# Other due times for the list scheduler of a one-core attention and two-layer kernel

## The chip, the core and the metric

The kernel runs on one core of one Trainium2 chip, as one program. The metric is the device time of that core in microseconds (us), the median over runs. A profile shows one execution: busy times of TensorE's matmuls (PE), of its weight loads (PEld), of VectorE (DVE), ScalarE (ACT), GpSimd (POOL), and of the DMA queue on SyncE (SP).

## The reference, cut to what matters

Sliding-window attention with a linear bias, and then two dense layers without any routing:

```python
B, H, S, D = 2, 8, 768, 64                       # q, k, v: float32
rel = pos[:, None] - pos[None, :]
keep = (pos[None, :] < 8) | ((rel >= 0) & (rel < 96))
scores = q @ k.T / 8 - slope[h] * dist           # dist: 96 for far global keys, else |rel|
a = softmax(where(keep, scores, -1e9))
x = (a @ v)  ->  1536 rows x 512
h = x @ w_in                                     # 512 x 2048
g = where(h >= 1, h, where(h <= -1, 0, (h + 1) ** 2 / 4))
x = g @ w_out                                    # 2048 x 512
h = x @ w_in2 ; g = maximum(0.01 * h, h) ; out = g @ w_out2
```

The weights arrive as 64-bit numbers, two 32-bit words each, and are put together on the chip.

## The kernel before

Every float32 operand of the dense layers is split into a high and a low part, `hi` and `lo`, and each product is taken as hi·hi, hi·lo and lo·hi. A hidden tile is 128 hidden units by up to 512 rows of `x`: 12 matmuls of 512 columns with the two parts of four pieces of 128.

The work is a list of operations. Each is put on it with `add(costs, fn, prio, after, takes, gives)`: what it would cost on each engine that may do it, the function that issues it, a priority, what must be done before, and the buffers that it takes from and gives back to rings. At build time `run()` (in `Schedule`) plays this list with the written costs: a free engine takes the ready operation with the smallest priority whose buffers are free, and its instructions are issued there and then. So the priority decides three things that stand fixed in the program afterwards: the order on each engine, which of several engines does an operation, and which buffer it gets. Where the player finds PE idle in the stretch up to the scores of the attention, it issues a dummy matmul on zeros (`dummy`, L369). Nothing is decided while the chip runs, except that an engine waits for what its next instruction needs.

The priority of an operation is a due time: the place of its tile in the play, plus an offset of its kind from the table `DUE` and some single constants:

```python
nms = [add({POOL: 2 * (pool_ts(W) + 83), DVE: 2 * (dve(W, True) + 62)}, nm(y), d + DUE["nm"] + y, [o7]) for y in range(2)]
due = due_of(c) + o * OUTLAG - JLEAD - (JTWO if m and not o else 0)
p2 = add({PE: c6}, prod(Ba, wa, 1, x0, 2, False, True), d + 2 * n7, [p1, cp, s_of[0, 2], s_of[0, 3]])
cc = add({DVE: dve(512)}, lambda e: V.tensor_tensor(out=Bc.tile, in0=Bb.tile, in1=S5.tile, op=ALU.add),
         d + 3 * n7 + 1400 + DUE["b0"], [p6, s5], ps=True)
p7 = add({PE: c6}, prod(Bb, wc, 0, lambda: xt[1], 0, False, False), d + 4 * n7, [cc] + x2_op["t3"])
```

The stages, and the names that come up again:

- **Attention**, 24 quads of four heads by 128 rows, `quad(i)`. PE transposes keys and queries (L559, `kd`, `qd`), the parts are taken from the bank (L220 or L222 for hi, L226 for lo), PE makes the scores (L591, `ks`, `qt`), VectorE adds the bias and finds the maximum (L600), ScalarE takes the exponent (L609), VectorE the reciprocal of the sum (L615), and the row is scaled, by VectorE (L622) or GpSimd (L624), which is operation `nm`. PE transposes the result (L633, `sm`) in two halves y = 0 and 1, and multiplies it with `v` (L646, `pT`, `vd`).
- **Weights**, `job(c, o)`: 16 tiles of `w_in` (o = 0) and of `w_out` (o = 1) for each layer, c = 0 to 31. A 512 KB load is followed by a chain that puts the words together: L438 or L440, L444, L448, L452 (VectorE alone; two inputs), L456 (ScalarE), L459 (a sum, VectorE or GpSimd), then the high part (L220 or L222) and the low part (L226 on VectorE, L228 on GpSimd).
- **Layer 1**, `step(s)`, 54 of them, the first ones between the quads: the hidden tile (L727), activation (L734, L742 or L744, L749), high and low part of the activated tile `g` (L220, and L226 or L228), the output product (L789).
- **Layer change**: the sums of layer 1 become the new `x`, and sums of its blocks become `xt` (L880, L226).
- **Layer 2**, `two(j, pair)`, j = 0 to 7, two weight tiles at a time. For two thirds of the rows seven products p1 to p7 stand in for eight (L921, 6 matmuls each), issued as p1, p5, p2, p6, p7, p3, p4. Between them a copy (cp, L220 or L222) is needed ahead of p2, a sum `cc` on VectorE (L966) ahead of p7, which also needs p6, and a second sum `ce` (L969) ahead of p4. The last third goes straight (L988). Activation is L932 and L937, the output product L1003, its sums L828, the last sums and the stores L846 and L849.

Of the kernel before, what the change touches and what calls it, by code (L numbers as in the profile page):

```python
# [55 lines left out]
class Schedule:  # L56
# [13 lines left out]
    def add(self, costs, fn, prio, after=(), takes=(), gives=(), tail=0.0, ps=False):  # L70

        o = Op()
        o.costs, o.fn, o.prio, o.gives, o.tail, o.ps = costs, fn, prio, gives, tail, ps

        o.takes = [(a, sum(b.ring is a.ring for b in takes[:y])) for y, a in enumerate(takes)]
        o.users, o.done, o.at = [], None, 0.0
        o.waits = 0
        for a in after:  # L80
            if a is not None and a.done is None:
                o.waits += 1
                a.users.append(o)
        self.ops.append(o)
        return o
# [91 lines left out]
def emit(tc, q, k, v, n_global, n_local, w_in1, w_out1, w_in2, w_out2, out, narrow):  # L177
# [25 lines left out]
    def act(n, psum=True):  # L203
        return (52 if psum else 93) + 0.833 * n

    def dve(n, fast=False):
        return 67 + (0.523 if fast else 1.044) * n
# [4 lines left out]
    def pool_ts(n):  # L212
        return 230 + 0.834 * n
# [10 lines left out]
    def sub(e, out_, a, b):  # L224
        if e == DVE:
            V.tensor_tensor(out=out_, in0=a, in1=b, op=ALU.subtract)  # L226
        else:
            GP.tensor_tensor(out=out_, in0=a, in1=b, op=ALU.subtract)  # L228

    def both(n):  # L230
        return {DVE: dve(n), POOL: pool_tt(n)}
# [48 lines left out]
    t_hid = []  # L280
    z = START
    units = PASSES[0]

    def quads(u):
        return range(u[0] // P * NQ, u[1] // P * NQ)

    for i in quads(units[0]):
        t_att[i] = START - STEP * (len(quads(units[0])) - i)
    for s, (m, g, u, f, first, last) in enumerate(seq):
        c = (u[1] - u[0]) * 10.15  # L290
        if m == 0 and g == 0 and u != units[-1]:
            after = quads(units[units.index(u) + 1])
            if first:
                seg = GROUPS[0] * c + len(after) * ATT
                for i in after:
                    t_att[i] = z + seg * (i - after[0] + 0.5) / len(after)
            c += len(after) * ATT / GROUPS[0]
        t_hid.append(z)
# [4 lines left out]
    t_two = []  # L303
    z -= TWO
    for j in range(NJ):
# [104 lines left out]
    def due_of(c):  # L410
        return t_hid[first_use[c]] if c < KF else t_two[(c - KF) // 2 * 2]

    jobs = sorted(((c, o) for c in range(NC) for o in range(2)), key=lambda j: (due_of(j[0]) + j[1] * OUTLAG, j[1]))
    w_t, w_op = {}, {}
    words = {}

    def job(c, o, prev):

        m, f = divmod(c, KF)
        due = due_of(c) + o * OUTLAG - JLEAD - (JTWO if m and not o else 0)  # L420
        R, Dd, Rr, W = Slot(raw), Slot(wd_r), Slot(wr_r), Slot(places[o])
# [42 lines left out]
        def s5(e):  # L464
            sub(e, W.tile[:, 1], Dd.tile.bitcast(F32), W.tile[:, 0].bitcast(F32))
        a = add({SP: 1460}, load, due + DUE["wl"], [prev], takes=[R], tail=DLAT)
        b = add({ACT: act(DM, False), DVE: dve(DM, True)}, s0, due + DUE["s0"], [a] + line("s0"), takes=[Dd])
        chain["s0"] = b
        b = add({POOL: pool_ts(DM), DVE: dve(DM, True)}, s01, due + DUE["s01"], [b])
        b = add({DVE: dve(DM, True)}, s1, due + DUE["s1"], [b])  # L470
        c1 = add({DVE: dve(DM)}, s11, due + DUE["s11"], [b])
        r = add({ACT: act(DM, False)}, s2, due + DUE["s2"], [a], takes=[Rr])
        e0 = add(both(DM), s3, due + DUE["s3"], [c1, r], gives=[Rr])
# [232 lines left out]
    def line(a):  # L706

        return [] if narrow else [chain.get(a)]
# [352 lines left out]
ABANKS = 6  # L1061
HBANKS = 3
SN = 1
JTWO = 4876.0
TWO = 6630.0
START = 547.0
STEP = 3638.0
ATT = 6076.0
OUTLAG = 10187.0
JLEAD = -3657.0  # L1070
DLAT = 2000.0

DUE = {'b0': 28848.0, 'b1': 29448.0, 'b2': 11048.0, 'b3': 11968.0, 'b4': -14334.0, 'bo': 42723.0, 'c1': 23764.0, 'c2': -19869.0, 'c3': -8113.0, 'c4': -7112.0, 'c5': -29972.0, 'c6': 58405.0, 'v': -15633.0, 'vg': 40229.0, 'a': -32879.0, 'half': 2.22, 'ld': -22756.0, 'tr': -4096.0, 'hi': -10213.0, 'lo': -27853.0, 'kg': -7231.0, 's': 12743.0, 'mx': -11641.0, 'ex': -9.0, 'rs': -70576.0, 'nm': -7377.0, 'ptr': -13975.0, 'pev': 10907.0, 'xmm': 9435.0, 'xhi': 9772.0, 'xlo': -2731.0, 'wl': -22500.0, 's0': -8192.0, 's01': -17963.0, 's1': 8642.0, 's11': -7299.0, 's2': 12279.0, 's3': 45224.0, 's4': -2838.0, 's5': -8589.0}


def load_words(nc, n_i, n_global, n_local):
# [140 lines left out]
```

## Time and profile before

| | |
|---|---|
| median of 3 runs | 622.96 us (622.67 to 623.07) |
| time of the profiled execution | 623.39 us |
| its span | 621.6 us |
| mean granted clock of TensorE in it | 0.997 |
| PE busy | 610.2 us, 98% of the span, 3404 matmuls |
| VectorE, ScalarE, GpSimd busy | 483.2, 352.6, 189.5 us |
| bytes moved | 46.98 MB |

The span runs from the first to the last instruction that the profile shows; the time holds 1.8 us more around it. PE is the engine that is nearly always busy, so time can be won or lost only where it waits, where it does work that isn't needed, or at the two ends of the program.

### The profile page before, as it was taken

The page shows a single profiled execution, that of the slowest core. Times are in us where ns is not written, and L with a number is a line of the kernel's source. Part 1 is how long each engine was busy: PE and PEld are TensorE (multiplying, and loading weights), DVE is VectorE, ACT ScalarE, POOL GpSimd, SP SyncE. Part 2 cuts the span into 40 slices and gives each one's busy share as a digit, 9 for nine tenths or more (in the row PEclk, how much of TensorE's full clock was granted, in tenths as well). Part 3 has the DMA queues.
Part 4 walks back from the last instruction along what each step waited for, and adds up shares of the span by engine and source line. Part 5 has one row for each costly group of instructions (what it writes and reads, how often), then busy time and mean ns, then how long its engine had stood idle before and what let it go on. Part 6 is the DMA issues. An engine that isn't in the chain of part 4 may idle for free.

```text
span 621.6 us, 9582 instructions
## 1 busy us (share of the span) xinstructions
PE 610.2 (98%) x3404; PEld 507.2 (82%) x3404; DVE 483.2 (78%) x1063; ACT 352.6 (57%) x755; POOL 189.5 (30%) x228
## 2 busy tenths in 40 slices
PE   9999999999999999999999999999999999999995
PEld 7888988888888888888888678888887888887884
DVE  6999899979994779823469999737989966988563
ACT  6999888966654456634445657524464533555300
POOL 3556634433220002200015052002545322556000
PEclk9999999999999999999999999999999999999998
DMA  9775344124331314400012103200232220220014
GB/s 188 191 171 128 84 129 99 46 69 135 106 114 54 101 35 141 131 1 1 0 35 67 35 34 103 67 1 1 67 108 80 85 67 2 68 69 1 2 59 150
DMA packets 61809, 46.98 MB, mean 76 GB/s; under 512 B 39608, under 2 KB 56248, under 8 KB 61752
## 3 DMA queue, kind: packets, MB, share of 16 engines
q1 hardware_dynamic: 61752, 46.28, 26.0%
q8 instruction: 29, 0.48, 0.3%
q14 instruction: 28, 0.23, 0.1%
HBM read 43.12 MB, written 3.15 MB: 74 GB/s over the span
## 4 chain that ended last, share of the span: by engine, by line


## 5 line engine op out<-in xcount | busy, mean ns | idle before, releaser
L789 PE MATMUL bank<-g,w 128*128 128x512 f32 (+1 forms) x648 | 141.7, 367 | 0.3 <-DVE g L226 0.3
L727 PE MATMUL bank<-x,w 128*128 128x512 f32 (+1 forms) x648 | 140.8, 367 | 0.4 <-DVE w L226 0.4
L789 PEld LDWEIGHTS bank<-g,w 128*128 128x128 f32 x648 | 112.3, 188 | 21.4 <-issue 0.9
L727 PEld LDWEIGHTS bank<-x,w 128*128 128x128 f32 x648 | 112.1, 188 | 21.2 <-DVE w L226 0.6
L828 DVE TENSOR_TENSOR part<-bank,part 128x512 f32<-128x512 f32 x96 | 63.6, 684 | 22.7 <-PE bank L1003 18.8
L1003 PE MATMUL bank<-w,g 128*128 128x512 f32 x312 | 80.5, 389 | 0.0
L459 POOL TENSOR_TENSOR wd<-wd,wr 128x512 int32<-128x512 int32 x36 | 49.6, 1377 | 87.5 <-DVE wd L452 73.0
L1003 PE MATMUL bank<-w,w 128*128 128x512 f32 x264 | 70.2, 389 | 0.0
L220 ACT CAST g<-t 128x512 fp32r<-128x512 f32 (+1 forms) x69 | 40.6, 591 | 49.3 <-PE bank L789 22.3
L1003 PEld LDWEIGHTS bank<-w,g 128*128 128x128 f32 x312 | 58.6, 188 | 12.2
L220 ACT CAST w<-wd 128x512 fp32r<-128x512 f32 x56 | 34.7, 620 | 45.2 <-POOL wd L459 12.4
L228 POOL TENSOR_TENSOR w<-wd,w 128x512 fp32r<-128x512 f32 x31 | 41.8, 1348 | 58.6 <-ACT w L220 32.6
L1003 PEld LDWEIGHTS bank<-w,w 128*128 128x128 f32 x264 | 49.5, 188 | 10.3
L734 ACT ACTIVATE t<-bank,half 128x512 f32<-128x512 f32 (+1 forms) x54 | 34.5, 640 | 41.3 <-PE bank L727 41.1
L226 DVE TENSOR_TENSOR g<-t,g 128x512 fp32r<-128x512 f32 (+1 forms) x60 | 42.2, 713 | 16.2 <-ACT g L220 16.0
L749 DVE SCALAR_TENSOR_TENSOR t<-bank,t 128x512 f32<-128x512 f32 (+1 forms) x54 | 33.8, 627 | 27.1 <-ACT t L742 26.6
L452 DVE SCALAR_TENSOR_TENSOR wd<-raw,wd 128x512 int32<-128x512 int32 x64 | 52.0, 812 | 1.5
L921 PE MATMUL bank<-x,w 128*128 128x512 f32 x192 | 48.4, 390 | 1.2 <-ACT bank L220 0.6
L444 POOL TENSOR_SCALAR wd<-wd 128x512 f32<-128x512 f32 x26 | 16.6, 643 | 107.0 <-ACT wd L438 93.2
L456 ACT ACTIVATE wr<-raw 128x512 int32<-128x512 uint32 x64 | 42.3, 670 | 11.9 <-DVE wd L459 10.7
L609 ACT ACTIVATE sm<-sm,st 128x256 f32<-128x256 f32 (+1 forms) x96 | 46.2, 489 | 0.1
L988 PE MATMUL bank<-x,w 128*128 128x512 f32 x192 | 45.1, 389 | 0.0
(115 smaller groups left out, 944.4 us busy)
## 6 DMA issues: line engine op xcount, KB each, us to landing
raw<-in_moe_w_in_dram SPq DMA_DIRECT2D x32, 512.0 KB, 3.7
raw<-in_moe_w_out_dram SPq DMA_DIRECT2D x32, 512.0 KB, 3.3
kd<-in_k_dram SPq DMA_DIRECT2D x24, 128.0 KB, 3.2
qd<-in_q_dram SPq DMA_DIRECT2D x24, 128.0 KB, 3.3
vd<-in_v_dram SPq DMA_DIRECT2D x12, 256.0 KB, 3.7
out_dram<-part SPq DMA_DIRECT2D x11, 256.0 KB, 2.1
out_dram<-part SPq DMA_DIRECT2D x2, 128.0 KB, 3.8
vg<-in_v_dram SPq DMA_DIRECT2D x2, 64.0 KB, 3.6
```

What stands on the lines that cost most here:

```text
L220: A.copy(out=out_, in_=in_)
L226: V.tensor_tensor(out=out_, in0=a, in1=b, op=ALU.subtract)
L452: V.scalar_tensor_tensor(out=Dd.tile, in0=hl()[0], scalar=-0x40000000, in1=Dd.tile, op0=ALU.bitwise_and, op1=ALU.bitwise_or)
L456: A.activation(out=Rr.tile, in_=hl()[1], func=AF.Copy, scale=2.0 ** -29)
L459: (V if e == DVE else GP).tensor_tensor(out=Dd.tile, in0=Dd.tile, in1=Rr.tile, op=ALU.add)
L609: A.activation(out=Sm.tile[:, a, 0:W], in_=Sm.tile[:, a, 0:W], func=AF.Exp, scale=-1.0, bias=St.tile[:, 0, a:a + 1], accum_out=St.tile[:, ...
L727: T.matmul(out=Hb.tile[:, 0:n], lhsT=wi.tile[:, a, kk * P:(kk + 1) * P], rhs=x[r][:, b, kk, c0:c0 + n], start=(kk == 0 and a + b == 0), st ...
L789: T.matmul(out=o[:, z * n:(z + 1) * n], lhsT=wo.tile[:, a, cc * P:(cc + 1) * P], rhs=Gt.tile[:, b, 0:n], start=st, stop=sp_)
L828: V.tensor_tensor(out=part[r][sl], in0=ac(), in1=part[r][sl], op=ALU.add)
L921: T.matmul(out=bank.tile, lhsT=w.tile[:, a, (2 * z + kk) * P:(2 * z + kk + 1) * P], rhs=xx()[:, b, kx + kk, :], start=st and kk == 0 and a ...
L988: T.matmul(out=Hb.tile, lhsT=w.tile[:, a, kk * P:(kk + 1) * P], rhs=x[2][:, b, kk, :], start=(kk == 0 and a + b == 0), stop=(kk == KD - 1 ...
L1003: T.matmul(out=Bo.tile, lhsT=Gt[z, r].tile[:, b, cb * P:(cb + 1) * P], rhs=wo[z].tile[:, a, :], start=(z == 0 and a + b == 0), stop=(z == ...
```

## The change

Only numbers of the table are replaced: seven single constants and the 41 offsets of `DUE`. No operation, cost, buffer ring or dependency is touched. The lines with single constants, and some of the offsets:

```diff
-JTWO = 4876.0
-TWO = 6630.0
-START = 547.0
-STEP = 3638.0
-ATT = 6076.0
-OUTLAG = 10187.0
-JLEAD = -3657.0
+JTWO = 5481.0
+TWO = 5365.0
+START = 1129.0
+STEP = 1441.0
+ATT = 6033.0
+OUTLAG = 9078.0
+JLEAD = -4197.0
```

What this does to the program is seen in the order of its instructions. In the pass that runs, PE has the same products, with 94 dummy matmuls in place of 90. VectorE has 27 instructions fewer, GpSimd 20 more, ScalarE 7 more. The order on PE differs up to about the 20th hidden tile of layer 1, is the same from there to the layer change, and differs again in parts of layer 2.

**First place: GpSimd, early in the attention.** The rows of GpSimd around the 30th; `sm` are the scores that `nm` scales (L624), `w_0_86` is the first tile of `w_in`, which the first hidden tile needs. Before:

```order
L624 TENSOR_SCALAR sm_124<-sm_124,st_127 128x256 x4
L222 CAST ks<-kg 128x4x32
L624 TENSOR_SCALAR sm_122<-sm_122,st_125 128x256 x4
L222 CAST ks<-kg 128x4x32
L459 TENSOR_TENSOR wd_82<-wd_82,wr_84 128x512
L624 TENSOR_SCALAR sm_124<-sm_124,st_127 128x256 x2
L744 TENSOR_TENSOR t_98<-t_98 128x256
```

After:

```order
L624 TENSOR_SCALAR sm_123<-sm_123,st_126 128x256 x2
L222 CAST ks<-kg 128x4x32
L459 TENSOR_TENSOR wd_82<-wd_82,wr_84 128x512
L222 COPY vd_116<-vg_118 32x512
L228 TENSOR_TENSOR w_0_86<-wd_82,w_0_86 128x512
L444 TENSOR_SCALAR wd_82<-wd_82 128x512
L624 TENSOR_SCALAR sm_122<-sm_122,st_125 128x256 x2
```

The low part of the first weight tile stood on VectorE (L226) and now stands on GpSimd (L228), with its sum (L459) earlier. The first hidden tile itself moves on PE from behind the sixth quad's product with `v` to behind the fourth's.

**Second place: VectorE at the layer change.** `g_95`, `g_96` and `g_97` are activated tiles of the last steps of layer 1, `w_1_91` is a weight tile, `t_98` and `t_99` are tiles in activation, `wd_82` a weight under way. L749 ends an activation and frees a bank. Before:

```order
L226 TENSOR_TENSOR xt_2100<-part_68,xt_2100 128x512 x2
L226 TENSOR_TENSOR w_1_91<-wd_82,w_1_91 128x512
L226 TENSOR_TENSOR g_97<-t_98,g_97 128x512
L226 TENSOR_TENSOR g_95<-t_99,g_95 128x512
L444 TENSOR_SCALAR wd_82<-wd_82 128x512
L448 TENSOR_SCALAR wd_82<-wd_82 128x512
L744 TENSOR_TENSOR t_98<-t_98 128x512
L749 SCALAR_TENSOR_TENSOR t_98<-bank_72,t_98 128x512
L749 SCALAR_TENSOR_TENSOR t_99<-bank_75,t_99 128x512
```

After:

```order
L226 TENSOR_TENSOR xt_2063<-part_68,xt_2063 128x512 x2
L226 TENSOR_TENSOR g_96<-t_99,g_96 128x512
L226 TENSOR_TENSOR g_95<-t_98,g_95 128x512
L226 TENSOR_TENSOR w_1_91<-wd_82,w_1_91 128x512
L744 TENSOR_TENSOR t_99<-t_99 128x512
L749 SCALAR_TENSOR_TENSOR t_99<-bank_77,t_99 128x512
L444 TENSOR_SCALAR wd_82<-wd_82 128x512
L749 SCALAR_TENSOR_TENSOR t_98<-bank_70,t_98 128x512
```

The two activated tiles now come ahead of the weight, and the first L749 ahead of the weight's next step. On ScalarE, at the same place, the copy cp and the last two activations of layer 1 now come ahead of weight steps.

**Third place: PE in the last pair, j = 7.** `x_66` and `xt` are the rows of the products (p6 is the row with `xt` and the weight `w_5`, p7 the next one with `xt`). Before:

```order
L921 MATMUL bank_71<-x_66,w_4_2102 128x512 x6
L921 MATMUL bank_70<-xt_2098,w_5_2103 128x512 x6
L1003 MATMUL bank_73<-w_2_92,g_94 128x512 x3
L1003 MATMUL bank_73<-w_7_2109,w_6_2108 128x512 x3
L921 MATMUL bank_70<-xt_2099,w_4_2102 128x512 x6
```

After:

```order
L921 MATMUL bank_71<-x_66,w_4_2065 128x512 x6
L921 MATMUL bank_70<-xt_2061,w_5_2066 128x512 x6
L1003 MATMUL bank_72<-w_0_90,w_3_93 128x512 x3
L1003 MATMUL bank_72<-w_1_91,g_97 128x512 x3
L1003 MATMUL bank_76<-w_0_90,w_3_93 128x512 x3
L1003 MATMUL bank_76<-w_1_91,g_97 128x512 x3
L921 MATMUL bank_70<-xt_2062,w_4_2065 128x512 x6
```

Between p6 and p7 there was one output product (six matmuls of L1003), and there are two now. In pair j = 4 two stand there before and after, but one further output product is moved ahead of that pair's p5.

## Rows read from the trace of the kernel before

**Rows 1.** The page: busy time by engine, with share of the span and count.
```profile
PE 610.2 (98%) x3404; PEld 507.2 (82%) x3404; DVE 483.2 (78%) x1063; ACT 352.6 (57%) x755; POOL 189.5 (30%) x228
```

**Rows 2.** Window of 40 to 60 us: length, busy (count) of PE, PEld, DVE, ACT, POOL, clock, DMA.
```profile
40.00:60.00 20.00, 19.00 (x197) 15.92 (x197) 19.72 (x77) 19.14 (x60) 10.59 (x19) 1.00 0.59 147
```

**Rows 3.** Timeline of PE, middle of layer 1: start, duration, engine, line, count.
```profile
253.87 2.88 PE L789 MATMUL bank<-g,w 128*128 128x512 f32 x12
256.58 2.88 PE L727 MATMUL bank<-x,w 128*128 128x512 f32 x12
```

**Rows 4.** Timeline, first hidden tile and quad 10; in brackets the idle time before.
```profile
42.12 0.50 PE L727 MATMUL bank<-x,w 128*128 128x256 f32 x2
43.06 1.45 PE L727 MATMUL bank<-x,w 128*128 128x256 f32 x10 [0.44 <-DVE w L226]
...
57.78 2.22 POOL L624 TENSOR_SCALAR sm<-sm,st 128x256 f32<-128x256 f32 x4 [3.54 <-DVE st L615]
57.91 0.67 PE L633 MATMUL bank<-ident,sm 128*128 128x128 f32 x4
59.13 0.66 PE L633 MATMUL bank<-ident,sm 128*128 128x128 f32 x4 [0.56 <-DVE x L226]
```

**Rows 5.** Timeline, layer change.
```profile
346.35 3.11 PE L789 MATMUL bank<-g,w 128*128 128x512 f32 x13
349.71 1.42 PE L789 MATMUL bank<-g,w 128*128 128x512 f32 x5 [0.26 <-DVE g L226]
350.98 1.53 PE L921 MATMUL bank<-x,w 128*128 128x512 f32 x6
351.70 1.29 DVE L749 SCALAR_TENSOR_TENSOR t<-bank,t 128x512 f32<-128x512 f32 x2
353.04 1.65 PE L921 MATMUL bank<-x,w 128*128 128x512 f32 x6 [0.54 <-DVE t L749]
354.69 0.57 ACT L220 COPY bank<-bank 128x512 f32<-128x512 f32 x1
355.32 1.65 PE L921 MATMUL bank<-x,w 128*128 128x512 f32 x6 [0.63 <-ACT bank L220]
...
359.53 2.88 PE L789 MATMUL bank<-g,w 128*128 128x512 f32 x12
362.80 1.65 PE L921 MATMUL bank<-xt,w 128*128 128x512 f32 x6 [0.38 <-DVE bank L966]
```

**Rows 6.** Timeline, pair j = 7, p6 and p7.
```profile
569.97 1.40 POOL L459 TENSOR_TENSOR wd<-wd,wr 128x512 int32<-128x512 int32 x1 [1.09 <-DVE wd L452]
570.25 1.66 DVE L452 SCALAR_TENSOR_TENSOR wd<-raw,wd 128x512 int32<-128x512 int32 x1
570.86 0.84 PE L1003 MATMUL bank<-w,w 128*128 128x512 f32 x3
571.84 0.68 DVE L966 TENSOR_TENSOR bank<-bank,s 128x512 f32<-128x512 f32 x1
572.58 1.65 PE L921 MATMUL bank<-xt,w 128*128 128x512 f32 x6 [0.88 <-DVE bank L966]
```

**Rows 7.** Timeline of PE, pair j = 4, between p6 and p7.
```profile
477.19 2.88 PE L1003 MATMUL bank<-w,g 128*128 128x512 f32 x12
480.20 1.67 PE L921 MATMUL bank<-xt,w 128*128 128x512 f32 x6
```

**Rows 8.** Timeline of PE, dummies and scores behind them; transposes and scores behind them.
```profile
7.25 2.02 PE L369 MATMUL bank<-zero 128*128 128x256 bf16 x17
9.19 1.32 PE L591 MATMUL bank<-ks,qt 64*128 64x256 f32 x12
...
44.35 1.04 PE L633 MATMUL bank<-ident,sm 128*128 128x128 f32 x8
45.31 0.86 PE L591 MATMUL bank<-ks,qt 64*128 64x256 f32 x10
```

**Rows 9.** Groups by line and shape: count, busy, mean ns of one, idle before.
```profile
L452 DVE SCALAR_TENSOR_TENSOR wd<-raw,wd 128x512 int32<-128x512 int32 x64 | 52.0, 812 | 1.5
```

More of the change, by code (lines that the diff above doesn't have):

```diff
@@ L1063 @@
 SN = 1
-JTWO = 4876.0
-TWO = 6630.0
-START = 547.0
-STEP = 3638.0
-ATT = 6076.0
-OUTLAG = 10187.0
-JLEAD = -3657.0
+JTWO = 5481.0
[5 more added lines that the diff above has]
+JLEAD = -4197.0
 DLAT = 2000.0
-DUE = {'b0': 28848.0, 'b1': 29448.0, 'b2': 11048.0, 'b3': 11968.0, 'b4': -14334.0, 'bo': 42723.0, 'c1': 23764.0, 'c2': -19869.0, 'c3': -8113.0, 'c4': -7112.0, 'c5': -29972.0, 'c6': 58405.0, 'v': -15633.0, 'vg': 40229.0, 'a': -32879.0, 'half': 2.22, 'ld': -22756.0, 'tr': -4096.0, 'hi': -10213.0, 'lo': -27853.0, 'kg': -7231.0, 's': 12743.0, 'mx': -11641.0, 'ex': -9.0, 'rs': -70576.0, 'nm': -7377.0, 'ptr': -13975.0, 'pev': 10907.0, 'xmm': 9435.0, 'xhi': 9772.0, 'xlo': -2731.0, 'wl': -22500.0, 's0': -8192.0, 's01': -17963.0, 's1': 8642.0, 's11': -7299.0, 's2': 12279.0, 's3': 45224.0, 's4': -2838.0, 's5': -8589.0}
+DUE = {'b0': 27487.0, 'b1': -7725.0, 'b2': 7698.0, 'b3': 18155.0, 'b4': -16724.0, 'bo': 42135.0, 'c1': 30472.0, 'c2': -36403.0, 'c3': -26250.0, 'c4': 9666.0, 'c5': -29309.0, 'c6': 42928.0, 'v': -18596.0, 'vg': 36984.0, 'a': -30449.0, 'half': 2.49, 'ld': -23578.0, 'tr': -1097.0, 'hi': -10704.0, 'lo': -25632.0, 'kg': -8445.0, 's': 6573.0, 'mx': -17624.0, 'ex': 167.0, 'rs': -86791.0, 'nm': -7267.0, 'ptr': -16954.0, 'pev': 11914.0, 'xmm': 6016.0, 'xhi': 12260.0, 'xlo': -7956.0, 'wl': -24180.0, 's0': -7248.0, 's01': -21914.0, 's1': 7880.0, 's11': -5575.0, 's2': 14164.0, 's3': 46641.0, 's4': -16435.0, 's5': 4613.0}
 def load_words(nc, n_i, n_global, n_local):
```

## The prediction

> **What bounds the kernel now.** I read the page's busy times first: PE works 98% of the span and VectorE 78%, so nothing but PE's own gaps can hold more than a per cent [rows 1]. Then I walked the timeline of PE from end to end and compared the distance between the starts of neighbouring blocks with what their matmuls need. In the middle of layer 1 twelve matmuls of 512 columns take 256.58 − 253.87 = 2.71 us, 0.226 each [rows 3]; a block whose distance to the next start is longer has waited by the difference. Idle time in brackets is less than that, since a pipelined PE drains while it waits.
>
> Seven waits come out of that walk, in four places, and nothing else above 0.2 us:
>
> - *First hidden tile*, 0.7: it starts at 42.12, does two matmuls, and goes on at 43.06 when VectorE has made the low part of its weight; 0.94 − 2 × 0.113 (256 columns) = 0.71 [rows 4].
> - *Quad 10*, 0.7: four transposes at 57.91, the next four at 59.13; at 0.12 each the first four need 0.48, so 0.74 is lost. The row blames VectorE's L226, but that is the last of several to signal; what the second half needs is `nm`, which GpSimd runs from 57.78 on [rows 4].
> - *Layer change*, four waits [rows 5]. 349.71 − 346.35 − 13 × 0.226 = 0.42, for the low part of an activated tile. 353.04 − 350.98 − 1.36 = 0.70, for p5, whose bank L749 gives back. 355.32 − 353.04 − 1.36 = 0.92, for p2, which needs the copy cp on ScalarE; about 0.13 of it is PE's restart after a stop (a block that starts after a stop lasts 1.65 and not 1.53). 362.80 − 359.53 − 2.71 = 0.56, for p7 and `cc`. With the restarts behind the first and the last (0.14 and 0.13) that is 2.87.
> - *Pair 4*, 0.4: 480.20 − 477.19 − 2.71 = 0.30, and 0.1 of a restart, p7 again [rows 7].
> - *Pair 7*, 1.15: 572.58 − 570.86 − 3 × 0.226 = 1.04 and 0.1 of a restart, p7 again: `cc` ran at 571.84 only, since the L452 ahead of it on VectorE lasted 1.66 [rows 6].
>
> Together 0.7 + 0.7 + 2.87 + 0.4 + 1.15 = 5.8 us, not quite 1% of the span. That is all a pure reordering can win from waits.
>
> **The change, part by part.** No operation is added or taken away but dummies, so every term is a wait that goes, stays or comes, or PE's own overhead.
>
> *The early attention.* The low part of the first weight stood on VectorE, which is busy 19.72 of 20 us there [rows 2]; now it is GpSimd's, with half of its time free, right behind its sum L459. PE meets the tile two quads earlier, which takes slack away again: between the two the low part is ready about a microsecond ahead by my count of GpSimd's work in the new order. `nm` of quad 10 goes to GpSimd alone, with a similar margin. I take both waits as gone: −1.4. If either comes back it costs its 0.7.
>
> *The layer change.* On VectorE the two low parts of `g` now stand ahead of the weight's. One L226 of 0.6 to 0.7 us leaves the way of the first wait of 0.42, which goes, with its restart: −0.56. p5 still needs its bank: the square of that step (L744) goes to GpSimd, which takes 1.40 for two inputs where VectorE takes 0.68 [rows 6], so L749 can't come much earlier. I leave 0.70 and add 0.3 and a restart: +0.4. The copy cp ran behind a weight's cast on ScalarE and started at 354.69; it now stands ahead of the weight's steps and can start when p1 is done. p1 ended by 352.51, p2 was due (without its wait) at 353.04 + 1.36 = 354.40, so 0.6 for the copy is covered: −0.92. `cc` waited for VectorE to clear a queue that is now shorter by a low part and two activations that GpSimd takes: −0.69. Sum −1.8; the bounds are 0 (all waits return in another form) and −2.87.
>
> *Pair 4.* One output product of six matmuls, 6 × 0.226 = 1.36 us, moves ahead of p5. VectorE and ScalarE have that much longer to prepare the pair's weights ahead of p6, and `cc` is not stuck behind them: −0.4, bounds 0 and −0.4.
>
> *Pair 7.* A second output product stands between p6 and p7, 1.36 us more of cover for a wait of 1.04: −1.15, with 0.3 to spare. If `cc` were held once more as long as there it would be late by about 0.7, so the lower bound of the gain is 0.4.
>
> *Dummies.* Four more, each (9.19 − 7.25) / 17 = 0.114 us [rows 8]: +0.45. Where PE would have waited anyway they cost nothing, so the bounds are 0 and 0.45; PE has no wait there in the trace of before, so I take the upper one.
>
> *Changes of the matmul's kind.* PE loses a little when the kind of tile changes: seven steps between transposes and the one to the scores take 45.31 − 44.35 = 0.96 [rows 8]; if seven take 0.11 like the dummies, the last is 0.2, some 0.1 too long. The new order has six such changes fewer (scores and products with `v` stand side by side more often): −0.6, bounds 0 and −0.6.
>
> *All other steps.* Some 60 instructions change their engine and nearly every quad has a new order. That every operation is on time again in such an order isn't to be hoped for. Bounds: nothing, and 5.8, as much as the order of before has. I take two waits of the mean size of the seven (5.8 / 7 = 0.83), rounded to +1.5.
>
> Sum: −1.4 − 1.8 − 0.4 − 1.15 + 0.45 − 0.6 + 1.5 = −3.4. The profiled execution took 623.39, which gives 620.0; it is 0.43 above the median of the runs shown, so the median should come to **619.6**.
>
> **One price weighed more closely.** The L452 of pair 7 began at 570.25, while GpSimd's L459 ran from 569.97 to 571.37, and lasted 1.66 [rows 6]. The mean of all 64 is 0.812 [rows 9], and one that meets nothing lasts about as long as the `cc` behind it, 0.68. So a two-input operation of VectorE that starts under one of GpSimd's is held for up to 0.98. The Trainium skill, page "SBUF — State Buffer", section "SBUF: two separate sides", says that VectorE and GpSimd share a pair of ports as an exclusive lock: whichever starts first has it for its whole instruction, and the other waits (VectorE when it has two inputs in SBUF against a GpSimd operation that reads SBUF). This row agrees: 1.66 is about the 1.12 left of L459 plus most of an own 0.68. It speaks against this change: by the rule the 20 instructions that go to GpSimd take VectorE's time as well as GpSimd's, up to the length of each, and the gain from moving them could turn into a loss; by the row that they are off VectorE's queue it couldn't.
>
> **Rivals.**
>
> *As many waits come as go.* For it: the new order is made by the same player from written costs, and the waits of before sit where a duration was not the written one (the L452 of 1.66). Nothing says that this happens less often in the new order. Against it: the walk through the new order shows cover at each of the old places. With 5.8 back in place of 1.5, the sum is +0.9 without margin to the dummies; with four or five new waits of 0.83 it is −4.9 + 4.5 × 0.83 = −1.2 to −0.4. I take −0.5, 622.5: no change that can be told.
>
> *Nothing comes in their place.* All named waits go and none comes: −4.9, a median of 618.1.
>
> *Slower: VectorE and GpSimd collide in the attention.* Place: 40 to 60 us, where VectorE has 0.28 us free in 20 and PE 1.0 [rows 2]. Each GpSimd operation with two inputs that now starts ahead of one of VectorE's may hold it for 0.98 us; with VectorE full, that delay goes on to every quad behind it until PE stops. Ahead of it is the margin of about a microsecond of the first tile and the 4.9 of terms that gain. Five collisions in the way of PE eat 4.9; from the seventh, 7 × 0.98 = 6.9, the kernel is 2 us slower than before, 625. Against it: scaling by `nm`, most of what moves in that stretch, has one input and no partner there, and of the 64 instructions of L452 together only 64 × (0.812 − 0.68) = 8.4 us are lost now in the whole kernel [rows 9], nearly all off the path.
>
> *The change does nothing.* That is the case of 622.5 by another road: PE is 98% busy, and the old waits may simply move by a block.
>
> **How the numbers follow.** A difference of 0.2%, 1.25 us, is about what a measurement of this kernel can tell from none. The forecast (618.6 to 621.5) gets 0.47; nothing in their place (617.5 to 618.6) 0.12; as many come as go (621.5 to 624.2) 0.26; slower by collisions 0.15. Faster by over 0.2% is below 621.7: 0.47 + 0.12 + 0.03 of the third = 0.62. Slower is above 624.2: 0.15. Same: 0.23. The range for 8 in 10 goes from 617.7, which leaves out 0.03, to 623.8, which leaves out the slower rival and the worst of the third case, 0.17.
>
> **What would show it.** In the profile after, the first hidden tile runs its twelve matmuls as one block; quad 10's transposes have no gap; at the layer change only p5 has a bracket; the blocks of p7 in pairs 4 and 7 have none. GpSimd's busy time is up by 15 to 25 us and VectorE's down by as much or less; if VectorE's busy time does not fall although it has 27 instructions fewer, collisions have eaten it. The prediction is wrong if the distances between PE's starts show more than two new waits, or if one is over 2 us, which would be a load or a weight chain that comes late and not a short operation.

## The result and the profile after

The kernel after takes **617.67 us** (median of 4 runs, 617.63 to 617.71) where the one before takes 623.02: a ratio of 0.9913, 95% interval 0.9898 to 0.9928. It is 5.35 us faster; 3.4 were forecast, and the range began at 617.7, which the median misses by 0.03.

Busy times of after, by engine, with the share of the span (615.8 us) and the count:

```profile
PE 607.2 (99%) x3408; PEld 507.2 (82%) x3408; DVE 474.5 (77%) x1036; ACT 354.4 (58%) x762; POOL 204.9 (33%) x248
```

GpSimd has 15.4 us more and VectorE 8.7 us less than in [rows 1]. The timeline of PE in after, at the layer change (start, duration, count, in brackets the idle time before):

```profile
344.81 4.24 PE L789 MATMUL bank<-g,w 128*128 128x512 f32 x18
348.89 4.28 PE L921 MATMUL bank<-x,w 128*128 128x512 f32 x18
353.01 1.52 PE L789 MATMUL bank<-g,w 128*128 128x512 f32 x6
...
355.73 2.88 PE L789 MATMUL bank<-g,w 128*128 128x512 f32 x12
358.68 1.66 PE L921 MATMUL bank<-xt,w 128*128 128x512 f32 x6
```

p1, p5 and p2 now stand in one block of 18 without a gap. All that is left of the 2.87 us of [rows 5] is 358.68 − 355.73 − 2.71 = 0.24 (twelve matmuls need 2.71 [rows 3]) in front of p7, and 0.1 for the restart. The timeline of after in pair 7, VectorE and PE, answers to [rows 6]:

```profile
568.19 1.66 DVE L452 SCALAR_TENSOR_TENSOR wd<-raw,wd 128x512 int32<-128x512 int32 x1
569.77 0.69 DVE L966 TENSOR_TENSOR bank<-bank,s 128x512 f32<-128x512 f32 x1
570.29 0.84 PE L1003 MATMUL bank<-w,g 128*128 128x512 f32 x3
570.98 1.52 PE L921 MATMUL bank<-xt,w 128*128 128x512 f32 x6
```

The collision is still there, L452 lasts 1.66 as before; `cc` ends at 570.46 and p7 is due at 570.98 only, since it has one output product more ahead of it. Pair 4 has no wait either: its p7 starts at 477.13, 2.71 behind the start of the twelve matmuls ahead of it, and that is what they need. In the attention the wait of quad 10 is gone and the first hidden tile runs as one block, but behind it is something new. The timeline of PE in after:

```profile
34.89 1.70 PE L727 MATMUL bank<-x,w 128*128 128x256 f32 x12
36.69 0.71 PE L633 MATMUL bank<-ident,sm 128*128 128x128 f32 x4
37.59 0.93 PE L633 MATMUL bank<-ident,sm 128*128 128x128 f32 x4 [0.20 <-DVE sm L622]
38.45 0.98 PE L591 MATMUL bank<-ks,qt 64*128 64x256 f32 x12
```

Twelve matmuls of 256 columns need 1.36 and have 1.80; four transposes need 0.48 and have 0.90 and 0.86. Three steps come late there, some 1.2 us together; the bracket names L622 of VectorE, which is `nm`.

**The start differs by execution.** Before the stages are compared, one thing has to be taken off. The second block of scores starts at another time in each profile, most of all because TensorE's clock rises from the lower of its two levels at another time, after dummies from 1.05 us on in each. The timelines of PE in before, in after, and in after run again:

```profile
4.65 0.63 PE L559 MATMUL bank<-ident,kd 128*128 128x128 f32 x2
11.04 0.98 PE L591 MATMUL bank<-ks,qt 64*128 64x256 f32 x12
343.62 2.88 PE L727 MATMUL bank<-x,w 128*128 128x512 f32 x12
```

```profile
4.42 0.38 PE L559 MATMUL bank<-ident,kd 128*128 128x128 f32 x2
10.37 0.98 PE L591 MATMUL bank<-ks,qt 64*128 64x256 f32 x12
342.10 2.88 PE L727 MATMUL bank<-x,w 128*128 128x512 f32 x12
```

```profile
4.66 0.63 PE L559 MATMUL bank<-ident,kd 128*128 128x128 f32 x2
10.78 0.97 PE L591 MATMUL bank<-ks,qt 64*128 64x256 f32 x12
```

The same two transposes take 0.63 or 0.38, and the two profiles of one program differ by 0.4 us at that point and by 0.4 us in their span (615.8 and 616.2). The clock is not all of it: in the first profile of after PE also waits 0.51 us for a load ahead of these scores. From there to the last hidden tile of layer 1 before takes 343.62 − 11.04 = 332.58 and after 331.73: **the attention, with layer 1, wins 0.85**. This repeats: the eight profiles with the old early numbers have 332.58 to 332.65 there, the seven with the new ones 331.73 to 331.84. The layer change wins 2.87 − 0.34 = **2.5**, pair 4 **0.4**, pair 7 **1.15**, which makes 4.9 of the 5.1 us by which the profiles differ apart from the start (5.8 in span less 0.67).

### The profile page after: what moved, and what is told of

Same layout as the page of the kernel before. It is cut to its first block, busy times and chain, and to the rows that moved or that the text cites. A ratio compares the mean times of both kernels' runs of the same rounds, so it can differ in the third digit from the quotient of the medians.

```text
span 615.8 us, 9602 instructions
## 1 busy us (share of the span) xinstructions
PE 607.2 (99%) x3408; PEld 507.2 (82%) x3408; DVE 474.5 (77%) x1036; ACT 354.4 (58%) x762; POOL 204.9 (33%) x248
## 4 chain that ended last, share of the span: by engine, by line
## 5 line engine op out<-in xcount | busy, mean ns | idle before, releaser
L789 PE MATMUL bank<-g,w 128*128 128x512 f32 (+1 forms) x648 | 141.3, 367 | 0.0
L789 PEld LDWEIGHTS bank<-g,w 128*128 128x128 f32 x648 | 112.6, 188 | 20.5 <-issue 0.7
L828 DVE TENSOR_TENSOR part<-bank,part 128x512 f32<-128x512 f32 x96 | 63.6, 686 | 27.3 <-PE bank L1003 23.2
L1003 PE MATMUL bank<-w,g 128*128 128x512 f32 x312 | 80.9, 389 | 0.0
L1003 PE MATMUL bank<-w,w 128*128 128x512 f32 x264 | 70.1, 389 | 0.0
L459 POOL TENSOR_TENSOR wd<-wd,wr 128x512 int32<-128x512 int32 x33 | 44.9, 1362 | 72.0 <-DVE wd L452 67.6
L1003 PEld LDWEIGHTS bank<-w,g 128*128 128x128 f32 x312 | 58.6, 188 | 12.2
L220 ACT CAST g<-t 128x512 fp32r<-128x512 f32 (+1 forms) x73 | 42.6, 585 | 41.2 <-PE bank L789 20.6
L220 ACT CAST w<-wd 128x512 fp32r<-128x512 f32 x61 | 37.8, 620 | 45.0 <-DVE wd L459 13.4
L228 POOL TENSOR_TENSOR w<-wd,w 128x512 fp32r<-128x512 f32 x32 | 42.5, 1332 | 52.3 <-ACT w L220 48.3
L1003 PEld LDWEIGHTS bank<-w,w 128*128 128x128 f32 x264 | 49.6, 188 | 10.3
L749 DVE SCALAR_TENSOR_TENSOR t<-bank,t 128x512 f32<-128x512 f32 (+1 forms) x54 | 33.9, 628 | 28.7 <-ACT t L742 28.1
L452 DVE SCALAR_TENSOR_TENSOR wd<-raw,wd 128x512 int32<-128x512 int32 x64 | 49.5, 774 | 1.7
L226 DVE TENSOR_TENSOR g<-t,g 128x512 fp32r<-128x512 f32 (+1 forms) x54 | 37.0, 692 | 16.5 <-ACT g L220 15.8
L921 PE MATMUL bank<-x,w 128*128 128x512 f32 x192 | 47.8, 390 | 0.0
```

The source lines that it names most:

```text
L220: A.copy(out=out_, in_=in_)
L452: V.scalar_tensor_tensor(out=Dd.tile, in0=hl()[0], scalar=-0x40000000, in1=Dd.tile, op0=ALU.bitwise_and, op1=ALU.bitwise_or)
L459: (V if e == DVE else GP).tensor_tensor(out=Dd.tile, in0=Dd.tile, in1=Rr.tile, op=ALU.add)
L789: T.matmul(out=o[:, z * n:(z + 1) * n], lhsT=wo.tile[:, a, cc * P:(cc + 1) * P], rhs=Gt.tile[:, b, 0:n], start=st, stop=sp_)
L828: V.tensor_tensor(out=part[r][sl], in0=ac(), in1=part[r][sl], op=ALU.add)
L921: T.matmul(out=bank.tile, lhsT=w.tile[:, a, (2 * z + kk) * P:(2 * z + kk + 1) * P], rhs=xx()[:, b, kx + kk, :], start=st and kk == 0 and a ...
```

## The experiments

Inserted lines shift the line numbers by up to 31: L922, L925, L949 and L952 are L921, L967 and L994 are L966, L997 is L969, L1031 is L1003, L776 and L779 are L749, L792 and L816 are L789, L252 is L226, L246 is L220, L486 is L459. "Before" is timed beside each on the same chip, 622.8 to 623.1. A wait is counted as in the prediction, by the distance of PE's starts.

**1 and 2. Half of the table each.** A copy of the table is used for the late operations, and which is which is exchanged:

```diff
+        DUE = DUE2 if m else globals()["DUE"]            # in job: m is the layer
+        DUE = globals()["DUE"] if s < 28 else DUE2       # in step
+        DUE = DUE2                                       # in sums and two
```

> The new numbers for the quads, the loads of v, the weights and the steps of layer 1 before the 28th; the old ones for everything later. Theory A (the time is won where PE's named waits stood, each stage by itself): only the attention's part is won, 11.8 - 9.9 = 1.9 us of PE's waits less 0.45 for four dummies, so about 1.5 us, 621.5 us; the layer change and the pairs 4 and 7 keep their waits of 2.9, 0.4 and 1.15. Theory B (the new early order leaves VectorE with more lead, and that is what clears the later waits): more than 3 us are won, 620 or less, and p5's wait at the layer change is gone here too.

> The opposite mix: the old numbers up to the 28th step of layer 1, the new ones behind it. Theory A: the layer change wins 2.6 of its 2.9 and the pairs 4 and 7 win 0.4 and 1.15, 4.2 in all, 618.8 us, and the first hidden tile and quad 10 still wait 0.7 each. Theory B: 2 us or less are won and p5 still waits.

early_only: 622.57 (0.999, 0.9981 to 0.9999). late_only: 618.49 (0.993, 0.9917 to 0.9944). The profile of early_only keeps every late wait and that of late_only has both early ones, with the 0.24 in front of p7 as its only late one. The timeline of PE in late_only:

```profile
349.50 4.26 PE L925 MATMUL bank<-x,w 128*128 128x512 f32 x18
...
356.32 2.88 PE L792 MATMUL bank<-g,w 128*128 128x512 f32 x12
359.28 1.66 PE L925 MATMUL bank<-xt,w 128*128 128x512 f32 x6
```

0.47 and 4.55 add up to 5.0. Theory A holds: the late numbers bring 4.55 of the 5.35 by themselves, and the early ones less than the 1.5 that were expected.

**3 and 4. Single operations moved.** The play is left as it is, and an operation's issue is put elsewhere in the list before it is written out:

```diff
+MOVES = [("job 17 1 s5", "behind", "step 51 a4")]
+            for a, where, b in moves:
+                y = issue.pop(at(a))
+                issue.insert(at(b) + (where == "behind"), y)
```

> The kernel before with one operation later on VectorE: the low part of the weight w_1_91 behind the two low parts of g at the layer change. Theory A1 (a wait that goes is won where it goes): the first wait of the layer change, 0.53, is won, 622.5 us. Theory A2 (passed on): that weight's buffer comes free 1.2 us later, L438 on ScalarE waits for it, and behind it on ScalarE stand the two activations L734 that p5's bank needs: the wait in front of p5 grows from 0.8 to 2 to 2.5, and the kernel is 0.6 to 1.2 us slower, 624.0.

> The kernel before with nine operations moved, and nothing else changed: at the layer change that low part, two activations ahead of L438 on ScalarE, L444 and L448 behind the second L749, the copy cp ahead of a weight's cast, cc ahead of a sum; in the pairs 4 and 7 cc ahead of one weight step. Theory A (the late gain sits in these few places): 2.4 of the layer change, 0.4 and 1.15, so 3.9 us are won, 619.1 us, with 0.4 to 0.5 left in front of p5. Rival (the waits are passed on along VectorE's full queue, and it takes a whole new order to be rid of them): less than 2 us, with waits elsewhere in layer 2.

In both, the low part of `w_1_91` (in nine_moves also that of one tile of `g`) is taken after its source has been written anew, so part of the values are others; what was expected of L438 waiting for that buffer could not happen. one_move: 623.44 (1.0007, 0.9998 to 1.0016). Its timeline of PE:

```profile
350.46 1.53 PE L949 MATMUL bank<-x,w 128*128 128x512 f32 x6
353.14 1.65 PE L949 MATMUL bank<-x,w 128*128 128x512 f32 x6 [1.15 <-DVE t L776]
```

The first wait is gone and p5's is 353.14 − 350.46 − 1.36 = 1.32 in place of 0.70: it was passed on whole. nine_moves took 623.31 (1.0006, 0.9997 to 1.0015); there PE lost 1.9 in front of p5, partly because the second low part of `g` had been put behind an activation and waited for it, so it decides nothing on p5. The next one has each operation behind all that it depends on.

**5 and 6. The same in two pieces.**

```diff
+    ("job 17 1 s5", "behind", "step 51 a4"), ("job 19 0 s0", "behind", "step 53 a2a"),
+    ("job 19 0 s1", "behind", "step 53 a2"), ("job 19 0 s01", "behind", "step 53 a2"),
+    ("two 0 1 <lambda>#0", "ahead", "job 18 0 s4"), ("two 0 1 <lambda>#2", "ahead", "sums 1 <lambda>#0"),
# and, in the other kernel
+    ("two 4 1 <lambda>#2", "ahead", "job 25 1 s1"), ("two 7 1 <lambda>#2", "ahead", "job 31 1 s11"),
```

> The kernel before with moves at the layer change alone, each behind all that it depends on: the low part of w_1_91 behind the two low parts of g, L438 behind the square of step 53 on ScalarE, L444 and L448 behind the second L749, the copy cp ahead of a weight's cast, cc ahead of a sum. Theory A (the waits of the layer change are local): the waits in front of the output product, p2 and p7 go, 0.45 stays in front of p5; 2.4 us are won, 620.6. Rival (passed on): the weight chain that is put back is late at one of the next products, and less than 1 us is won, 622.1 or more, with a new wait of over 0.5 us within 50 us behind the layer change.

> The kernel before with two moves: in pair 4 cc ahead of the two steps L448 and L452 of one weight, in pair 7 cc ahead of one L452. Theory A (local): both waits go, 0.4 and 1.15, and the weights they put back have cover; 1.5 us are won, 621.5. Rival (passed on): the weights are late at the output products behind them, and the waits come back there; under 0.5 us is won.

layer_moves: 622.94 (0.9999, 0.999 to 1.0008). Its timeline of PE:

```profile
349.80 1.52 PE L949 MATMUL bank<-x,w 128*128 128x512 f32 x6
351.59 3.06 PE L949 MATMUL bank<-x,w 128*128 128x512 f32 x12 [0.27 <-DVE t L776]
...
380.32 2.88 PE L1031 MATMUL bank<-w,g 128*128 128x512 f32 x12
384.46 1.66 PE L949 MATMUL bank<-xt,w 128*128 128x512 f32 x6 [1.26 <-DVE bank L994]
385.96 1.52 PE L949 MATMUL bank<-x,w 128*128 128x512 f32 x6
387.95 1.65 PE L949 MATMUL bank<-xt,w 128*128 128x512 f32 x6 [0.46 <-DVE bank L997]
```

All went at the layer change as forecast, 351.59 − 349.80 − 1.36 = 0.43 left in front of p5. But p7 of pair 1 now waits 384.46 − 380.32 − 2.71 = 1.43, and p4 behind it 0.63, where the kernel before waits for nothing. The rival holds: the 2.4 us are given back 33 us later. cc_moves: 621.83 (0.998, 0.9971 to 0.9989), 1.2 won; pair 7 is clean, and in pair 4 the wait of 0.3 moved from p7 to p4. So the wait of pair 7 was local; that of pair 4 came back, smaller, at its next product, and those of the layer change in pair 1. That fits a VectorE which was late there as a whole; no run shows that by itself.

**7 and 8. More work on VectorE than the order knows of.**

```diff
-            V.scalar_tensor_tensor(out=Dd.tile, in0=hl()[0], ...)
+            for _ in range(2 if m and narrow else 1):
+                V.scalar_tensor_tensor(out=Dd.tile, in0=hl()[0], ...)
```

> The kernel before with L452 done twice for each of the 32 weight tiles of layer 2 (the second time gives the same bits), so 32 times 0.69 us more on VectorE, which the order knows nothing of. Theory R (the old order has less cover for durations other than the written ones): it loses 2 us or more more than the kernel after does with the same load. Rival (PE has as much cover in either order, and the old one only has its waits in unlucky places): both lose the same within 1 us.

> The kernel after with the same load, L452 twice for each weight tile of layer 2. Theory R: it loses less than hold_before by 2 us or more, and the waits in front of p7 in pairs 1 to 7 stay under 0.5 us each. Rival: the same loss as hold_before within 1 us.

hold_before: 645.06, 22.1 us slower than before (1.0354, 1.0339 to 1.0368); hold_after: 637.82, 20.2 slower than after (1.0236 of before, 1.0218 to 1.0253). The added work is 32 × 0.69 = 22.1 us: nearly all of it reaches PE in either order. The 1.9 between them lies short of theory R's 2 and outside the rival's 1, and the runs of hold_after alone spread over 3.0 us (635.65 to 638.65), so neither theory is decided; a general cover for other durations is not what the new order has. Part of the cost is the clock, in both: the granted clock of 480 to 500 us is 0.91. The timeline of PE in hold_before:

```profile
491.48 2.93 PE L922 MATMUL bank<-xt,w 128*128 128x512 f32 x6 [3.35 <-DVE bank L967]
494.21 1.64 PE L922 MATMUL bank<-x,w 128*128 128x512 f32 x6
```

After 3.35 us of idling six matmuls take 2.93 and not 1.65: TensorE's clock has fallen to its lower level.

**9 and 10. The later p7, and cc once more, on the kernel after.**

```diff
+    ("two 1 1 fn#4", "ahead", "two 0 1 mm#2"), ("two 7 1 fn#4", "ahead", "two 6 1 mm#2"),
# and, in the other kernel
+    ("two 0 1 <lambda>#2", "ahead", "sums 1 fn#1"),
```

> The kernel after with p7 of the pairs 1 and 7 one output product earlier on PE, where the old order has it, and nothing else moved. Theory C (the later p7 is the cover, cc comes as late as ever): in the profile of after cc ends at 382.55 in pair 1 and 570.46 in pair 7, and p7 would be due at 381.94 and 569.62, so PE waits 0.6 and 0.85 there, with a restart of 0.1 each, and the kernel is 1.7 us slower than after, 619.3. Rival (VectorE is ahead in the new order and the later p7 is not needed): no wait, 617.7.

> The kernel after with one move: cc of pair 0 ahead of two sums and a low part of g on VectorE, which takes 1.1 us off its way to the last wait of the layer change, 0.34 with its restart. If that wait is local 617.3 us; if it is passed on to p7 of pair 1, where cc has 0.75 us of slack and the sums of its weights come 0.69 later, it turns up there and nothing is won, 617.7.

uncover: 620.59 (0.9957 of before, 0.9944 to 0.9971), 2.9 slower than after. Its timeline of PE:

```profile
383.04 1.65 PE L949 MATMUL bank<-xt,w 128*128 128x512 f32 x6 [0.50 <-DVE bank L994]
...
387.46 1.66 PE L949 MATMUL bank<-xt,w 128*128 128x512 f32 x6
...
572.11 1.66 PE L949 MATMUL bank<-xt,w 128*128 128x512 f32 x6 [0.73 <-DVE bank L994]
```

p7 waits 0.66 and 0.89 as theory C has it, and p4 waits 0.2 in each pair besides, which was not expected; with restarts 2.4, and the rest of the 2.9 is a start 0.35 later and the spread of the runs. So the output product that stands ahead of p7 is the cover in pairs 1 and 7. after_cc: 618.0 (0.9914 of before, 0.99 to 0.9927), no gain that the runs can tell: the 0.34 are gone and 0.23 are in front of p7 in pair 1.

**11 and 12. Every offset shifted at random.** Of the 40 offsets of `DUE` (40, and not the 41 named above), all but `half` get a random number of −300 to 300 ns, drawn once for each of the two kernels.

> The kernel before with each offset of its table changed by a random number of up to 300 ns, which gives another order nearly everywhere. Theory N (an order taken near the old one has as many waits as it has, in other places): PE's waits of over 0.2 us behind the first 20 us sum to 4 to 8 us, and the time is within 2 us of 623.0. Theory S (the old table was picked for the order that it gives, and any other order is worse): 9 us of waits or more, 626 us or more.

> The kernel after with each offset changed by a random number of up to 300 ns, which again gives another order nearly everywhere. Theory N (what the new numbers have is a region of orders with few waits): 1 to 3 us of waits over 0.2 us, the time within 1.5 us of 617.7. Theory S (it is the one order that has few): 5 us of waits or more, 621.5 us or more.

jitter_before: 627.25 (1.0061, 1.0044 to 1.0078); jitter_after: 625.32 (1.0025, 1.0014 to 1.0035). By the time theory S holds, but the places split it. In layer 2 the waits of jitter_before are those of before one by one (0.40, 0.70, 0.79, 0.55, 0.26, 1.00), and jitter_after has the one 0.24 of after. All the rest is in the attention: up to the last hidden tile of layer 1 jitter_before takes 5.7 us longer than before, jitter_after 6.9 longer than after. A part of that is the clock, which falls behind the longest waits (granted 0.83 from 60 to 70 us in both). The waits look like this, in a timeline of PE in jitter_after:

```profile
59.64 1.09 PE L646 MATMUL bank<-pT,vd 128*64 128x128 f32 x16
61.53 0.44 PE L633 MATMUL bank<-ident,sm 128*128 128x128 f32 x2 [0.79 <-POOL sm L624]
62.66 0.44 PE L633 MATMUL bank<-ident,sm 128*128 128x128 f32 x2 [0.70 <-POOL sm L624]
```

**13 and 14. One sum on the other engine.** What gave VectorE its lead at the layer change is in the rows ahead of it. The timelines of GpSimd and VectorE in before (the last row is ahead of `cc`), and of VectorE in after:

```profile
337.60 1.75 POOL L459 TENSOR_TENSOR wd<-wd,wr 128x512 int32<-128x512 int32 x1
338.12 1.79 DVE L226 TENSOR_TENSOR x<-part,x 128x512 fp32r<-128x512 f32 x1
...
360.01 1.78 DVE L226 TENSOR_TENSOR g<-t,g 128x512 fp32r<-128x512 f32 x1
```

```profile
336.58 0.68 DVE L226 TENSOR_TENSOR x<-part,x 128x512 fp32r<-128x512 f32 x1
...
349.33 0.68 DVE L749 SCALAR_TENSOR_TENSOR t<-bank,t 128x512 f32<-128x512 f32 x1
...
356.99 0.69 DVE L226 TENSOR_TENSOR g<-t,g 128x512 fp32r<-128x512 f32 x1
```

In before the L226 of `x` meets a weight's L459 on GpSimd and lasts 1.1 us longer; in after that sum is VectorE's, later, and L749 gives p5's bank back at 350.01, 0.24 ahead of need. The low parts of `xt`, the last long block of VectorE ahead of the layer change, start 1.14 us behind the start of the last hidden tile in before and 0.01 behind it in after. A second L226 of before, at 360.01, is held by an L228 just ahead of `cc` and p7's wait; in after it is not. That one was not tried by itself. Here only the engine of the first sum, and with it its place, is exchanged:

```diff
+    ("job 18 0 s3", "on", DVE), ("job 18 0 s3", "ahead", "job 18 0 s4"),      # before
+    ("job 18 0 s3", "on", POOL), ("job 18 0 s3", "ahead", "step 53 a2a"),     # after
```

> The kernel before with one operation on another engine: the sum L459 of one weight tile, which GpSimd runs from 337.60 in the profile of before, goes to VectorE behind the low part of step 52. Theory P (that sum holds VectorE: the L226 of x beside it lasts 1.79 and not 0.68, and the 1.1 us of lead are what the layer change lacks): the L226 lasts 0.7, the first wait of the layer change, 0.42, and p5's, 0.70, go; the copy's 0.8 in front of p2 stays; the L459 takes 0.68 ahead of cc, so p7's wait stays near 0.5; 1.0 to 1.3 us are won there. Rival (p5 waits for the order on VectorE and ScalarE): p5 waits 0.7 as before.

> The opposite on the kernel after: the same sum back on GpSimd, ahead of the square of step 53. Theory P: GpSimd starts it some 9 us before its place in the play, the L226 of x lasts 1.8 again, VectorE has 1.1 us less lead, and p5, whose bank came free 0.24 ahead of need, waits 0.6 to 0.9; with the restart 0.7 to 1.0 us slower there. Rival: p5 doesn't wait, and the time is that of after.

s3_gpsimd: 619.22 (0.9941 of before, 0.9928 to 0.9955), 1.6 slower than after run beside it (617.64); from the last hidden tile of layer 1 on its profile takes 274.62 us and that of after 273.74, so 0.9 of the 1.6 arise there. Its second block of scores also starts 0.3 to 0.7 later than in the two profiles of after. Its timelines of VectorE and PE:

```profile
337.26 1.78 DVE L252 TENSOR_TENSOR x<-part,x 128x512 fp32r<-128x512 f32 x1
...
349.58 1.52 PE L952 MATMUL bank<-x,w 128*128 128x512 f32 x6
351.93 3.00 PE L952 MATMUL bank<-x,w 128*128 128x512 f32 x12 [0.82 <-DVE t L779]
```

The collision is back and p5 waits 351.93 − 349.58 − 1.36 = 0.99: theory P, with the held sum and the wait in one trace; the low parts of `xt` are 1.12 behind again. s3_vector: 623.06 (1.0007, 0.9998 to 1.0016). Its timelines of ScalarE and PE:

```profile
353.71 0.62 ACT L246 CAST w<-wd 128x512 fp32r<-128x512 f32 x1 [1.13 <-DVE wd L486]
354.81 0.58 ACT L246 COPY bank<-bank 128x512 f32<-128x512 f32 x1
...
350.42 3.16 PE L952 MATMUL bank<-x,w 128*128 128x512 f32 x12
355.44 1.66 PE L952 MATMUL bank<-x,w 128*128 128x512 f32 x6 [1.86 <-ACT bank L246]
```

The first wait is gone and 0.3 with a restart is left of p5's 0.70 (its block of twelve lasts 3.16 and not 2.88), which bears theory P out on the old order too. But the copy cp stands behind the cast that needs the moved sum, and p2 waits 2.0. From the output product ahead of p1 to the start of p2 PE loses 2.3 us in all where it loses 2.2 in before, so nothing is won: three waits have become one.

**15 and 16. Fewer dummies, and after once more.**

```diff
+        count.append(0)
+        if len(count) > 41:
+            return
         T.matmul(out=still.tile[:, 0:FILLN], ...)
```

> The kernel after without the 53 dummy matmuls that come behind the first 41 (from 11.8 us on), everything else in its order. Theory D (a dummy costs its 0.114 us): 6 us are won, 611.7. Rival (they stand where PE would wait for loads, VectorE or ScalarE anyway): within 1 us of after, and the four dummies that the change adds cost nothing; if the granted clock falls in the gaps, slower by what the matmuls at the lower clock take longer.

> The kernel after, unchanged, on the same chip as the three beside it: 617.7, and the start of the second block of scores, 10.4 us in its first profile and 10.1 to 11.0 in the others, tells how much of a difference between two profiles is where TensorE's clock rose. If the medians of one kernel differ by no more than 0.3 us the start matters little.

after_again: 617.64 (617.39 to 618.1), within 0.03 of the first median, so the start moves a profile more than a median. few_dummies: 618.95 (0.9936 of before, 0.9922 to 0.9949), 1.3 us *slower* without 53 of them. Windows of few_dummies and of after (length, busy of PE, PEld, VectorE, ScalarE and GpSimd, then the granted clock):

```profile
10.00:20.00 10.00, 8.25 (x63) 5.75 (x62) 9.29 (x50) 9.73 (x38) 2.58 (x7) 0.83 1.16 250
20.00:30.00 10.00, 9.98 (x86) 7.22 (x86) 8.11 (x37) 8.63 (x29) 4.09 (x10) 0.83 0.54 141
```

```profile
10.00:20.00 10.00, 10.00 (x102) 8.32 (x101) 9.37 (x51) 9.45 (x39) 3.26 (x9) 1.00 1.13 245
20.00:30.00 10.00, 10.00 (x106) 8.14 (x106) 9.54 (x40) 9.67 (x33) 4.73 (x11) 1.00 0.73 193
```

PE waits in place of the dummies (1.7 us ahead of the transposes at 16.20), the clock falls to the lower level until about 24 us, and the last hidden tile of layer 1 comes 1.2 us later behind the second scores than in after. Theory D falls: together the 53 save more than they cost. That one of them costs nothing this run doesn't show.

## Why the prediction was wrong

- **The waits that go.** The walk along PE's starts found all of them. It lists eight waits in five places, where the prediction says seven in four (5.8 / 8 = 0.73 and not 0.83; two of them still round to 1.5). Seven went, and p7's at the layer change fell from 0.56 to 0.24. Pair 4 (−0.4) and pair 7 (−1.15) came as worked out, with the mechanism of pair 7 as told: cover, not a collision less (uncover). That of pair 4 was not tried by itself.
- **The layer change, "I leave 0.70 and add 0.3 and a restart: +0.4".** This is the step that failed: p5 waits 0 in after, −0.70 in place of +0.4. The size was taken from the square that goes to GpSimd. What decides is that VectorE comes to this place 1.1 us earlier, because one L459 leaves GpSimd and an L226 is no longer held; s3_gpsimd puts it back and gets 0.99 of wait. On the other side p7, with its restart, won 0.35 and not 0.69. Layer change in all: −2.5 and not −1.8. The prediction weighed collisions as a rival that makes the new order slower and priced one of the old order, in pair 7; it did not look for one 14 us ahead of p5's wait.
- **"All other steps", +1.5.** New waits of about 1.2 came, all at one place of the attention, three short steps behind the first hidden tile; in layer 2 none came (its 0.34 is the rest of an old wait). So the size is near, but by luck: the mean of the old waits had been put on two unnamed ones. By the prediction's own sign, more than two new waits, it was wrong here.
- **The early terms.** −1.4, +0.45 and −0.6 with new waits of 1.2 would give −0.35, and −0.85 was measured. Added up over PE's starts from the second scores to the last hidden tile, the four dummies bring +0.44, the steps at a change of kind −0.9, and all else, the waits gone and come, −0.4. Steps of some 0.20 us at such a change are 83 in after and 89 in before, so the six fewer are there. None of this was tried by a run of its own.
- **The sum.** −0.85 − 2.5 − 0.4 − 1.15 = −4.9, against −3.4: 0.7 of the difference is the layer change, the rest lies in the early part. The rival with nothing in their place, 618.1, came nearest by its number, not by its mechanism, since new waits did come. The 0.43 by which the profiled execution of before lay above its median is of the size of the spread at the start.
- **The slower rival** did not come: VectorE has 8.7 us less to do and L452 lasts 0.774 on the mean and not 0.812 [rows 9]. Its price is not a fixed one: an L226 or L452 that starts under an operation of GpSimd lasts some 0.55 longer than what is left of that, 1.79 with 1.23 left and 0.80 with 0.25 left. Two inputs are not the condition: none of the 43 L828 of before that start under one, with one input in a bank, lasts over 0.69, while an L448 of after, with one input, lasts 1.33 and not 0.42 (at 349.93, under an L228), and an L622 0.57 and not 0.32 (at 37.46, under an L624). So `nm`, which the prediction took to have no partner, does collide, if only for 0.25. The Trainium skill, page "SBUF — State Buffer", section "SBUF: two separate sides", calls this an exclusive lock for a whole instruction. The rows agree: L459 ends at 339.35, and the L226 that began at 338.12 ends 0.56 later, not much less than its own 0.68.

What stays open: which of the early numbers bring the 0.85, whether an early order without the new 1.2 us is to be had, how much of p7's gain at the layer change is the second held L226, and whether the order of layer_moves and the engine of s3_vector together would win on the old order what the new numbers win; that was not run.

## What to carry to other kernels

A wait taken away by a local move need not be won: look at the next place where the same engine is waited for (layer_moves gave 2.4 us back 33 us later, one_move and s3_vector at once; cc_moves kept 1.2). An order fixed at build time does not fix when an engine starts: GpSimd ran a sum long before its place in the play (in the list it stands beside the L749 of 351.70 [rows 5], it started at 337.60) and held VectorE just where its lead was needed, so look for operations of 1.7 us in place of 0.7 in the rows ahead of a wait, not only at it. And waits of a new order are not to be priced by the mean of the old ones where the layers differ: in the one draw for each kernel, small shifts of the due times left those of layer 2 as they were and made new ones in the attention.

## What the runs showed of the hardware

The time at which TensorE's clock first rises differs by execution of one program (the first two transposes, at 4.42 and 4.66 us, take 0.38 in one profile of after and 0.63 in the other), and with it the start of all that stands behind: in the profiles here the second block of scores starts between 10.10 us (late_only) and 11.04 (before, which has the same early numbers). A load that comes later is part of it in some.

53 dummy matmuls that look like 6 us of waste (53 × 0.114 [rows 8], an estimate) keep the granted clock at 1.00 from 10 to 30 us; without them it is 0.83 there, and the program is 1.3 us slower.

An L226 or L452 of VectorE, two inputs in SBUF, that starts while GpSimd works on an operation of its own lasts until 0.53 to 0.56 us behind that operation's end, wherever more than 0.15 us of it are left: 32 times in before, 21 in after. One with an input in a bank (L828) is not held, 43 times in before.
